# Other rows of the query weights in each partition, and a smaller step in the transposes of x

## The chip, the cores and the metric

The kernel runs on one core of a Trainium2 chip. The metric is the device time of one execution in microseconds; lower is better. The core has five engines with their own instruction streams: PE (matrix multiply, with its weight loads shown apart as PEld), DVE (vector), ACT (scalar), POOL (GpSimd) and SP, whose queue issues most of the transfers here.

## The reference

A block of new tokens attends to the last window of a key and value cache, with eight query heads for each head of keys and values. In sizes: x is 8 x 32 x 1024, the caches are 8 x 4 x 8192 x 128, of which the last W = 2048 positions are used, wq is 1024 x 4096 and wo is 4096 x 1024, all in bf16.

```python
q = (x @ wq).reshape(B, Sq, Hq, Dh).transpose(0, 2, 1, 3)
k = repeat(k_cache[:, :, Sk - W:, :], 8, axis=1)
v = repeat(v_cache[:, :, Sk - W:, :], 8, axis=1)
p = softmax(einsum("bhqd,bhkd->bhqk", q, k) * Dh ** -0.5)
o = einsum("bhqk,bhkd->bhqd", p, v)
out = o.transpose(0, 2, 1, 3).reshape(B, Sq, Hq * Dh) @ wo
```

## The kernel before

The attention is worked off in 32 units, one for each of 4 groups (a head of keys and values with its 8 query heads) and 8 batches. In each unit PE multiplies the transposed keys by the queries (line 504, 4 matmuls of 256 columns a step), ACT takes the exponential (line 506), and PE multiplies the result by the values, which carry an extra column of ones for the sum of the exponentials (line 515). Between these steps a plan written out by hand, in slots of a quarter of a unit, places the other work of PE: the queries of the next group (line 285), the transposes of keys, and the output projection (line 322). The order of instructions on each engine is that of the source; no scheduler moves them.

The contraction of x @ wq runs over the 1,024 columns of x. It is cut into 8 chunks of 128, one row of wq to a partition in each chunk. Any assignment of rows to chunks and partitions gives the same sum, as long as x is cut in the same manner. Before the change, partition p holds rows 8p to 8p+7 of wq: chunk c is row 8p+c. The weights of a group are loaded in two halves, chunks 0 to 3 and 4 to 7, each into its own tile `wq_sb` (`load_wq`, line 168). Every half is cut further into pieces of one or two chunks, each one transfer on SP's queue.

At the start (`start`, from line 340 on) the transfers go out in this order: x in two parts (SP and ACT), the first four chunks of group 0 one by one, chunks 4 and 5 together, half of the first keys, chunks 6 and 7 one by one, the other half of the keys, then values and further keys.

PE begins with eight warm-up matmuls on constants (line 375), since nothing has landed yet. It then transposes x in 16 blocks of 128 x 128 (`x_turn`, line 383, in two halves of 8), and two copies for each half, on DVE and ACT (line 386), bring them to `xT`. For each chunk, 8 matmuls (line 405, one for each head) follow, with 16 transposes of the first keys (line 397) before and after the last two chunks. Only then does the first unit start. The queries of half the batches for heads 4 to 7 are made a little later (line 301).

The transposes read x with a step, to match the rows of the weights: chunk c takes every eighth column, beginning at c.

```python
nc.tensor.transpose(ps[:, c, t, :], x_sb[:, t, half * H + c:self.D:self.DC], self.ident[:, :])
```

Here H is 4 and DC is 8. A weight load of PE takes these 128 columns, so that neighbours lie 8 elements, 16 bytes, apart in a partition.

Of the kernel before, what the change touches and what calls it, by code (L numbers as in the profile page):

```python
# [108 lines left out]
class Fast:  # L109
# [50 lines left out]
    def load_wq(self, g, half, cuts=(2, 2)):  # L160

        P, GW = self.P, self.rep * self.Dh

        def piece(i, n):
            if i == 0:
                self.wq_t[g, half] = self.wp.tile([P, self.DC // 2, GW], BF16, name="wq_sb", tag="w")
            c0 = half * self.DC // 2 + i
            self.nc.sync.dma_start(out=self.wq_t[g, half][:, i:i + n, :],  # L168
                                   in_=self.wq[:, g * GW:(g + 1) * GW].rearrange("(p c) n -> p c n", p=P)[:, c0:c0 + n, :])
        return [lambda i=sum(cuts[:k]), n=n: piece(i, n) for k, n in enumerate(cuts)]  # L170

    def load_wo(self, gq):
# [166 lines left out]
    def start(self):  # L339
        nc, P = self.nc, self.P  # L340
        warm = self.ps_s.tile([P, 512], FP32, name="warm_ps", tag="s_ps")
        one = nc.const_aps.tensor
        x_sb = self.vp.tile([P, self.NT, self.D], BF16, name="x_sb", tag="v")
        xf = self.x.rearrange("b s d -> (b s) d")
        H = self.DC // 2
# [33 lines left out]
        def x_turn(half, pl, tag):  # L379
            ps = pl.tile([P, H, self.NT, P], BF16, name="xT_ps", tag=tag)  # L380
            for c in range(H):
                for t in range(self.NT):
                    nc.tensor.transpose(ps[:, c, t, :], x_sb[:, t, half * H + c:self.D:self.DC], self.ident[:, :])
            for i, copy in ((0, nc.vector.tensor_copy), (1, nc.scalar.copy)):
                c0 = half * H + i * H // 2
                copy(out=self.xT[:, c0:c0 + H // 2, :], in_=ps[:, i * H // 2:(i + 1) * H // 2, :, :].rearrange("p c t s -> p c (t s)"))

        x_turn(0, self.ps_m, "m")
        x_turn(1, self.ps_s, "s_ps")
        qs = [self.ps_o.tile([P, 2, self.NQ], FP32, name="q0_ps", tag="o_ps") for _ in range(2)]  # L390
        qs.append(self.ps_m.tile([P, 4, P], FP32, name="q0_ps", tag="m"))
# [302 lines left out]
```

## Time and profile before

| | |
|---|---|
| median of 4 runs | 184.8 us (184.49 to 185.19) |
| profiled execution, its own time | 184.5 us |
| its span, first to last instruction | 182.7 us |
| DRAM read over the span | 41.42 MB, 230 GB/s |
| weights of the queries, transfers | 13 of 512 KB, 6 of 256 KB |
| transposes of x (line 383) | 16, first and last start at 4.4 and 5.8 us |
| first matmul of the queries (line 405) | 6.01 us |

The page gives, for each engine, its busy time, the share of the span and the number of instructions. PE and PEld overlap. The chain of waits follows the last instruction back to what released each step; in its pieces the first number is the start in us, the second the length. A row of windows shows the stretch, its length, the busy time of PE, PEld, DVE, ACT and POOL with the number of instructions, then the granted clock of PE, the DMA engines' share and GB/s. An issue row gives the size and the time from issue to landing.

### The profile page before, as it was taken

Reading aid. Unit: us, or ns where it says so; the run is one execution under the profiler, and the core shown is the slowest. Engines: PE = TensorE matmul, PEld = TensorE weight load, DVE = VectorE, ACT = ScalarE, POOL = GpSimd, SP = SyncE. Lnnn points to the kernel's source line nnn. Section 1 sums busy time; section 2 is a strip of 40 time slices with the busy share of each in tenths; the row PEclk is TensorE's granted clock in tenths of the full one; section 3 lists DMA queues with packets and bytes.
Section 4 is the critical chain, followed back from the end, with each engine's and each line's share of the span. In section 5 each row is a group of like instructions: output and inputs, shape, how many; then the busy total and the mean of one; then the engine's idle time right before and its main releaser. Section 6 shows DMA issues by size and latency. Waiting matters only on the chain.

```text
span 182.7 us, 5015 instructions
## 1 busy us (share of the span) xinstructions
PE 177.4 (97%) x2026; PEld 152.5 (83%) x2041; DVE 126.0 (69%) x257; ACT 136.0 (74%) x146; POOL 89.1 (49%) x138
## 2 busy tenths in 40 slices
PE   8989999999999999999999999999999999999993
PEld 2889999999999999998777899988787788888853
DVE  0228899679887698487799566777587987554253
ACT  2218898898897888997777787888877788888800
POOL 2004465069870795945939807929705949600000
PEclk9999999999999999999999999999999999999999
DMA  5999999999999999999999999999989999970013
GB/s 188 341 413 406 240 385 355 221 305 262 373 390 246 343 207 369 351 320 318 286 388 357 401 253 262 372 229 367 315 248 286 358 250 374 212 210 0 0 40 85
DMA packets 52954, 51.73 MB, mean 283 GB/s; under 512 B 39744, under 2 KB 40256, under 8 KB 52928
## 3 DMA queue, kind: packets, MB, share of 16 engines
q1 hardware_dynamic: 52352, 50.90, 97.9%
q10 hardware_dynamic: 576, 0.49, 0.9%
q8 instruction: 16, 0.26, 0.6%
q14 instruction: 10, 0.08, 0.1%
HBM read 41.42 MB, written 0.52 MB: 230 GB/s over the span
## 4 chain that ended last, share of the span: by engine, by line
PE 93%; DMA 4%; SPq 1%; issue 1%; DVE 0%
PE o_ps L515 32%; PE s_ps L504 31%; PE op_ps L322 14%; PE q_ps L285 11%; DMA wq_sb<-in_wq_dram 4%; PE q_ps L405 2%; PE ql_ps L301 1%; PE tp L244 1%; SPq L168 1%; PE kf_ps L397 0%; SPq L347 0%; DVE o_t L332 0%; PE cnt_ps L570 0%
## 5 line engine op out<-in xcount | busy, mean ns | idle before, releaser
L506 ACT ACTIVATE pT<-s_ps 128x1024 bf16<-128x1024 f32 x128 | 128.4, 1027 | 26.9 <-PE s_ps L504 26.7
L270 POOL TENSOR_SCALAR kTv<-kb 32x512 bf16<-32x512 bf16 x126 | 84.3, 669 | 51.6 <-DVE kb L259 33.4
L515 PE MATMUL o_ps<-va,pT 128*128 128x129 bf16 x1024 | 78.8, 220 | 0.1
L515 PEld LDWEIGHTS <-pT 128*128 128x128 bf16 x1024 | 68.5, 98 | 3.1
L504 PE MATMUL s_ps<-QT,kT 128*128 128x256 bf16 x336 | 50.4, 272 | 0.1
L504 PEld LDWEIGHTS <-kT 128*128 128x128 bf16 x336 | 31.9, 98 | 9.4
L322 PE MATMUL op_ps<-wo_sb,OT 128*128 128x512 bf16 (+2 forms) x129 | 32.8, 353 | 0.6
L259 DVE STREAM_TRANSPOSE kb<-k_raw 128x512 bf16<-128x512 bf16 x44 | 29.7, 692 | 1.1 <-DMA k_raw<-in_k_cache_dram 0.8
L285 PE MATMUL q_ps<-xT,wq_sb 128*128 128x256 bf16 x192 | 28.3, 273 | 0.0
L439 DVE COPY va<-v_sb 128x2048 bf16<-128x2048 bf16 x30 | 25.3, 844 | 2.0 <-DMA v_sb<-in_v_cache_dram 1.6
L504 PE MATMUL s_ps<-QT,kTv 128*128 128x256 bf16 x176 | 26.4, 273 | 0.1
L445 DVE RECIPROCAL RL_all<-o_ps 128x2 f32<-128x2 f32 x32 | 5.3, 166 | 26.8 <-PE o_ps L515 26.5
L268 DVE COPY kTv<-kb 32x512 bf16<-32x512 bf16 x50 | 22.7, 455 | 1.2
L504 PEld LDWEIGHTS <-kTv 128*128 128x128 bf16 x176 | 17.0, 98 | 6.1
L285 PEld LDWEIGHTS <-wq_sb 128*128 128x128 bf16 x192 | 16.9, 98 | 1.2
L451 DVE STREAM_TRANSPOSE OT<-o_sb 128x256 bf16<-128x256 bf16 x32 | 14.3, 446 | 1.1
L449 DVE TENSOR_TENSOR o_sb<-o_ps,RL_all 128x256 bf16<-128x256 f32 x32 | 13.6, 424 | 1.1
L322 PEld LDWEIGHTS <-OT 128*128 128x128 bf16 x144 | 11.4, 98 | 2.3 <-DVE OT L451 0.2
L437 POOL TENSOR_SCALAR va<-v_sb 128x2048 bf16<-128x2048 bf16 x2 | 3.8, 1897 | 17.2 <-DMA v_sb<-in_v_cache_dram 17.2
L288 ACT CAST QT<-q_ps 128x512 bf16<-128x512 f32 x12 | 7.0, 583 | 0.2 <-PE q_ps L285 0.2
L329 DVE TENSOR_TENSOR oacc<-op_ps,oacc 128x512 f32<-128x512 f32 x8 | 5.3, 662 | 2.0 <-PE op_ps L322 2.0
L405 PE MATMUL q_ps<-xT,wq_sb 128*128 128x256 bf16 (+1 forms) x64 | 5.8, 246 | 0.9 <-DMA wq_sb<-in_wq_dram 0.9
(35 smaller groups left out, 43.1 us busy)
## 6 DMA issues: line engine op xcount, KB each, us to landing
v_sb<-in_v_cache_dram SPq DMA_DIRECT2D x30, 512.0 KB, 6.8
wo_sb<-in_wo_dram SPq DMA_DIRECT2D x16, 512.0 KB, 6.7
wq_sb<-in_wq_dram SPq DMA_DIRECT2D x13, 512.0 KB, 6.6
k_raw<-in_k_cache_dram SPq DMA_DIRECT2D x13, 512.0 KB, 5.8
wq_sb<-in_wq_dram SPq DMA_DIRECT2D x6, 256.0 KB, 5.0
v_sb<-in_v_cache_dram SPq DMA_DIRECT2D x4, 256.0 KB, 5.0
kT<-in_k_cache_dram SPq DMA_TRANSPOSE x36, 7.3
k_raw<-in_k_cache_dram SPq DMA_DIRECT2D x2, 256.0 KB, 6.7
```

The costliest lines, as they stand in the source:

```text
L259: nc.vector.transpose(out=st["kb"][:, sl, :], in_=self.k_raw[ui][:, sl, :])
L268: nc.vector.tensor_copy(out=out, in_=in_)
L270: nc.gpsimd.tensor_scalar(out=out, in0=in_, scalar1=1.0, scalar2=1.0, op0=ALU.mult, op1=ALU.mult)
L285: nc.tensor.matmul(st[k][:, hl % 2, :], lhsT=self.wq_t[g, i][:, c % (DC // 2), hl * P:(hl + 1) * P], rhs=self.xT[:, c, :], start=(c == 0 a ...
L322: nc.tensor.matmul(ps[:, 0:w], lhsT=self.OT[:, gq, c, t * P:(t + 1) * P], rhs=self.wo_t[gq][:, c, n0:n0 + w], start=(k == 0), stop=(k == 7))
L405: nc.tensor.matmul(ps, lhsT=self.wq_t[0, c // H][:, c % H, h * P:(h + 1) * P], rhs=self.xT[:, c, 0:n], start=(c == 0 and h in (0, 2, 4)), ...
L439: self.nc.vector.tensor_copy(out=out, in_=in_)
L449: nc.vector.tensor_tensor(out=o_sb[:, :, :, :], in0=o_ps[:, :, 0:Dh].rearrange("p q (i c) -> p q c i", c=4), in1=rl[:, ui * QT_N:(ui + 1) ...
L451: nc.vector.transpose(out=self.OT[:, g * QT_N:(g + 1) * QT_N, :, b * self.Sq:(b + 1) * self.Sq], in_=o_sb[:, :, :, :])
L504: nc.tensor.matmul(s_ps[:, jj, :], lhsT=self.kT[ui][:, c * CJ + jj, :], rhs=q_u, start=True, stop=True)
L506: nc.scalar.activation(out=pT[:, :, :], in_=s_ps[:, :, :], func=ACT.Exp, bias=0.0, scale=self.scale)
L515: nc.tensor.matmul(o_ps[:, qt, 0:self.VW], lhsT=pT[:, jj, qt * P:(qt + 1) * P], rhs=va[:, j, 0:self.VW], start=(j == 0 and qt == 0), stop= ...
```

## The change

In each half of the weights (512 rows of wq), partition p takes rows 4p to 4p+3 of that half. Chunk c of half h is then row 512h + 4p + c, where it was row 8p + 4h + c. The columns of x follow: the transposes of half h read every fourth column of the 512 columns of that half, so neighbours in a weight load lie 8 bytes apart. A transfer still moves the same number of rows of 2 KB; the rows of two neighbouring partitions lie 32 KB apart in DRAM, where they were 64 KB apart. No instruction is added, removed or moved.

```diff
@@ load_wq, piece
-            c0 = half * self.DC // 2 + i
+            R = self.D // 2
             self.nc.sync.dma_start(out=self.wq_t[g, half][:, i:i + n, :],
-                                   in_=self.wq[:, g * GW:(g + 1) * GW].rearrange("(p c) n -> p c n", p=P)[:, c0:c0 + n, :])
+                                   in_=self.wq[half * R:(half + 1) * R, g * GW:(g + 1) * GW].rearrange("(p c) n -> p c n", p=P)[:, i:i + n, :])
@@ start, x_turn
-                    nc.tensor.transpose(ps[:, c, t, :], x_sb[:, t, half * H + c:self.D:self.DC], self.ident[:, :])
+                    nc.tensor.transpose(ps[:, c, t, :], x_sb[:, t, half * H * P + c:(half + 1) * H * P:H], self.ident[:, :])
```

## The prediction

> **What bounds the kernel now.** I read the page's busy shares first, then the chain of waits over the first 16 us, then PE's own waits, and last the transfers of the first 12 us one by one.
>
> ```profile
> PE 177.4 (97%) x2026; PEld 152.5 (83%) x2041; DVE 126.0 (69%) x257; ACT 136.0 (74%) x146; POOL 89.1 (49%) x138
> PE q_ps L405 <- DMA wq_sb<-in_wq_dram: 0.9, 1, 0.9
> 3.07 6.55 DMA wq_sb<-in_wq_dram
> 9.67 1.49 PE q_ps L405 x16
> 11.16 0.45 PE kf_ps L397 x8
> 11.61 1.32 PE q_ps L405 x16
> ```
>
> PE is busy 97% of the span. The second line is from the list of PE's waits, which has only one other entry, the 0.8 us before the warm-ups: one wait of 0.9 us for the query weights of group 0. From the third line on (chain of waits: start, length, what) the chain is a transfer until 9.62 us and PE work after that, to the end. So the time is the landing of one transfer (x chunks 4 and 5 of the first query weights, issued at 3.07) plus 173 us of PE work that the change does not touch. The change touches two things: how PE reads x in the 16 transposes, and which rows of DRAM the weight transfers read.
>
> **The transposes (line 383).** Rows of the timeline, PE's weight loads: start, length, what.
>
> ```profile
> 1.59 0.15 PEld L375 LDWEIGHTS <-const-bfloat16-1.0 128*128 128x128 bf16 x1 [0.28 <-issue]
> 2.02 0.15 PEld L375 LDWEIGHTS <-const-bfloat16-1.0 128*128 128x128 bf16 x1 [0.28 <-issue]
> ...
> 4.65 0.38 PEld L383 LDWEIGHTS <-x_sb 128*128 128x128 bf16 x3
> ...
> 5.50 0.34 PEld L383 LDWEIGHTS <-x_sb 128*128 128x128 bf16 x4
> ...
> 10.95 0.49 PEld L397 LDWEIGHTS <-k_raw 128*128 128x128 bf16 x8
> ...
> 6.01 2.80 PE L405 MATMUL q_ps<-xT,wq_sb 128*128 128x256 bf16 x32
> 9.67 1.05 PE L405 MATMUL q_ps<-xT,wq_sb 128*128 128x256 bf16 x10 [0.86 <-DMA wq_sb<-in_wq_dram]
> ...
> 141.46 0.86 PE op_ps L322 x4
> ```
>
> In the source's rows one load of x takes 164 ns (median), one of k_raw 98. Three loads of x in 0.38 us start (0.38 - 0.164)/2 = 0.108 us apart; the later four, overlapping, (0.34 - 0.15)/3 = 0.063; the eight of k_raw, contiguous, (0.49 - 0.098)/7 = 0.056. The change halves the step of x from 16 to 8 bytes. What is that worth? [...] The warm-up matmuls of 512 columns start 0.43 us apart (1.59, 2.02), while four of 512 columns late in the chain of waits (last line above) take 0.86 us, 0.215 each: PE ran at half pace until at least 4.3 us, although the profile's clock row shows 1.00 there. Half of 0.43 by a quarter of the columns is 0.108 for 128 columns, exactly what the early transposes show, and the same 16-byte step then runs at 0.063. The clock sets the early pace, not the step. [...]
>
> [...] The 32 matmuls of chunks 0 to 3 run from 6.01 to 8.81, and then PE waits 0.86 us. [...] Also the copies of xT move forward with the transposes and end in the same wait. Cost of this part: 0.
>
> **The weight transfers (line 168).** The number of transfers, their sizes, their order on SP's queue, the bytes per packet (2 KB, since a group is 1,024 of 4,096 columns) and the order of instructions on every engine stay the same. A one-row piece reads 128 packets; before they lie 64 KB apart over the whole 8 MB matrix, after 32 KB apart over one half of it. Whether DRAM minds is what no row shows directly, so I bound it. Each issue, with KB and us from issue to landing (issues start at 1.19, 1.66, 2.12, 2.60, 3.07, 3.55 for the first half of k_raw, 4.50, 4.87):
>
> ```profile
> wq_sb<-in_wq_dram SPq DMA_DIRECT2D x1, 256.0 KB, 3.8
> wq_sb<-in_wq_dram SPq DMA_DIRECT2D x1, 256.0 KB, 4.6
> wq_sb<-in_wq_dram SPq DMA_DIRECT2D x1, 256.0 KB, 4.8
> wq_sb<-in_wq_dram SPq DMA_DIRECT2D x1, 256.0 KB, 5.3
> wq_sb<-in_wq_dram SPq DMA_DIRECT2D x1, 512.0 KB, 6.5
> k_raw<-in_k_cache_dram SPq DMA_DIRECT2D x1, 256.0 KB, 6.7
> wq_sb<-in_wq_dram SPq DMA_DIRECT2D x1, 256.0 KB, 6.5
> wq_sb<-in_wq_dram SPq DMA_DIRECT2D x1, 256.0 KB, 6.8
> ...
> 5.00:6.00 1.00, 1.00 (x13) 0.92 (x12) 0.42 (x1) 0.01 (x1) 0.00 (x0) 1.00 0.91 285
> 10.00:11.00 1.00, 1.00 (x15) 0.94 (x13) 0.00 (x0) 0.00 (x0) 0.00 (x0) 1.00 1.06 412
> ```
>
> Landings: 5.0, 6.3, 6.9, 7.9, 9.6 (chunks 4 and 5), 10.3 (k_raw), 11.0, 11.6. The last steps, for k_raw, chunk 6 and chunk 7, are all near 0.67 us for 256 KB: the 64 KB pitch then costs nothing against k_raw's contiguous rows. But from 5.0 to 9.6, five such amounts landed in 4.6 us instead of 5 x 0.67 = 3.35: 1.25 us were lost at the start, and the two window rows (last columns: DMA share and GB/s) show it as 285 GB/s between 5 and 6 us against 412 at 10 to 11. The trace does not say whether the pitch, or simply the start, caused that. Ends: if the pitch caused all of it and 32 KB cures it, chunks 4 and 5 land 1.25 sooner, of which PE can use its 0.86 wait and about 0.1 of earlier start, so -0.95; if the new pattern makes the second half pay it again, +0.7 (below). I take 0, because chunks 6 and 7 have the pitch and pay nothing, so time since the start looks like the cause, not the address.
>
> The other 12 transfers of weights, 512 KB each, land well ahead: those of group 1 issued at 20.66 and 21.29 take 5.9 and 6.5 us, so they are there at 26.6 and 27.8, and the first matmul on them starts at 29.3. That is cover of 1.5 us; each would need to take a good half longer than it does before PE sees it.
>
> **The sum.** The profiled execution took 184.5 us, 182.7 of them span. Transposes 0, transfers 0, no instruction moved: 184.5 again, which stands 0.3 below the median of 184.8. My forecast on the median's scale is 184.8.
>
> **The rivals.**
>
> *The transfers get faster.* The weights' 1.25 us at the start are partly due to the 64 KB pitch. For: the loss falls on weights, and between 3 and 4 us, while x (contiguous) was still coming in, the windows show 383 GB/s. Against: chunks 6 and 7. Anything from 0.55 to 0.95 us comes off: 183.85 to 184.25, say 184.1. It cannot be more: at 8.8 PE is the bound.
>
> *The second half becomes a first read (slower).* Before, chunk c of any partition lies in the same 64 KB that chunk 0 touched, so half 1 reads neighbours of what was just read. After, half 1 is another 4 MB that nothing has touched. If being touched for the first time is what chunks 1 to 3 paid (6.9 and 7.9 against steps of 0.67: 2.9 us for three, 0.3 extra each), chunks 4 and 5 land about 0.6 later, and since PE has no cover there, every bit of it reaches the end; chunks 6 and 7 add 0.6 more against cover of 0.4 (chunk 6 lands at 11.0, and PE takes it after the keys' transposes, at 11.4), so 0.1 to 0.2 on top: +0.7 to +0.8, 185.5. It decides as soon as chunks 4 and 5 land later than 9.6, with no threshold; beyond 0.55 us it is measurable. Against: chunk 0 itself, the first touch of all, lands at 5.0, only 0.6 after x (0.74 + 3.7 = 4.4), so it shows no stretch.
>
> *The pitch hurts all weights (slower).* If 32 KB makes engines collide and each 512 KB takes twice its 1.3 us step, group 1 arrives 2.6 later against cover of 1.5: +1.1 there, with another +1 at the start: 187. Against: smaller pitch, nearer to the contiguous case.
>
> That the change does not do what it says I exclude: step and rows are plain in the source.
>
> **How the numbers follow.** What a measurement of this kernel can tell from no change is about 0.3%, 0.55 us (the four runs alone lie 0.7 apart). Forecast, nothing visible: 0.40, all within. Faster transfers: 0.30, faster. Second half paying again: 0.25; pitch hurting everywhere: 0.05; both slower. The range 183.9 to 185.7 takes in the whole of the gain, the forecast with its spread, and most of the first slower case; it leaves out the last and the far end of the one before. The likeliest case alone is 184.3 to 185.3.
>
> **What would show it.** Right: line 383's early loads still 0.107 apart and the late ones nearer 0.056, xT copied a little earlier, PE's wait for the weights before L405 grown by that much, and chunks 4 and 5 landing at 9.6 within 0.3. The faster rival: that wait gone and the transfer's piece in the chain ending near 8.8. The first slower one: the wait at 1.4 us or more, with the later landings spaced over 0.67. The last: waits of PE for wq_sb at line 285. My forecast is wrong if chunks 4 and 5 land over half a microsecond away from 9.6, or if early transposes drop to 0.06 and the time moves with them.

## The result and the profile after

The changed kernel takes 184.3 us in the median of 34 runs (183.64 to 186.31), the kernel before 184.88 in 55 runs of the same comparison. The ratio is 0.997, with a 95% interval of 0.9956 to 0.9983: 0.3% faster, at the edge of what I had called measurable, and I had forecast no visible difference. Three repeats of the same comparison gave less (1.0004, 0.9984, 0.9981). What follows is therefore about two questions: is it faster, and which of the two edits does it.

The page of the changed kernel, its busy line:

```profile
PE 177.4 (97%) x2026; PEld 152.4 (84%) x2041; DVE 125.9 (69%) x257; ACT 136.0 (75%) x146; POOL 89.3 (49%) x138
```

The same 177.4 us of PE: no work has become shorter. PE's list of waits, the entry for the weights:

```profile
PE q_ps L405 <- DMA wq_sb<-in_wq_dram: 0.3, 1, 0.3
```

The wait that was 0.9 is 0.3. The chain of waits of the changed kernel, at its start and its end (start, length, what):

```profile
3.08 5.98 DMA wq_sb<-in_wq_dram
9.11 1.49 PE q_ps L405 x16
...
175.36 3.94 PE op_ps L322 x34
```

and the last line's counterpart in the kernel before:

```profile
175.92 3.94 PE op_ps L322 x34
```

Chunks 4 and 5 land at 9.06 where they landed at 9.62. PE goes on at 9.11 instead of 9.67, 0.56 earlier, and the last block of the output projection also starts 0.56 earlier. In between nothing is lost and nothing is gained in these two executions (in two others of those below, part of such a gain is lost again). The span fell by 0.4 only (182.7 to 182.3), because the last stores took a little longer in this execution.

The issues of the changed kernel, in the order shown for before (size, us from issue to landing):

```profile
wq_sb<-in_wq_dram SPq DMA_DIRECT2D x1, 256.0 KB, 3.9
wq_sb<-in_wq_dram SPq DMA_DIRECT2D x1, 256.0 KB, 4.4
wq_sb<-in_wq_dram SPq DMA_DIRECT2D x1, 256.0 KB, 4.6
wq_sb<-in_wq_dram SPq DMA_DIRECT2D x1, 256.0 KB, 5.1
wq_sb<-in_wq_dram SPq DMA_DIRECT2D x1, 512.0 KB, 6.0
```

Chunks 1 to 5 each come 0.2 to 0.6 us sooner; the first does not. One window of the changed kernel (last columns: DMA share, GB/s):

```profile
5.00:6.00 1.00, 1.00 (x14) 0.90 (x12) 0.42 (x1) 0.02 (x1) 0.00 (x0) 1.00 1.05 397
```

Between 5 and 6 us, where before moved 285 GB/s, there are now 397. One such row proves little: the kernel with the old rows and the new step, shown below, moved 367 in the same microsecond. The transposes, on the other hand, give nothing to the end. From the source's rows of line 383 and the timeline:

```profile
L383 PEld LDWEIGHTS <-x_sb x16: 112/138/147, 4.4 to 5.7; 128*128 128x128 bf16 x16
```
```profile
4.37 1.64 PE L383 MATMUL xT_ps<-ident,x_sb 128*128 128x128 bf16 x16
6.00 2.80 PE L405 MATMUL q_ps<-xT,wq_sb 128*128 128x256 bf16 x32
```

A load is 26 ns shorter (138 against 164), the 16 transposes take 1.64 us instead of 1.69, and the first matmul of the queries starts at 6.00 instead of 6.01.

### The profile page after: what moved, and what is told of

Same layout as the page of the kernel before. It is cut to its first block, busy times and chain, and to the rows that moved or that the text cites. A ratio compares the mean times of both kernels' runs of the same rounds, so it can differ in the third digit from the quotient of the medians.

```text
span 182.3 us, 5015 instructions
## 1 busy us (share of the span) xinstructions
PE 177.4 (97%) x2026; PEld 152.4 (84%) x2041; DVE 125.9 (69%) x257; ACT 136.0 (75%) x146; POOL 89.3 (49%) x138
## 4 chain that ended last, share of the span: by engine, by line
PE 93%; DMA 3%; SPq 1%; issue 1%; DVE 0%
PE o_ps L515 32%; PE s_ps L504 31%; PE op_ps L322 14%; PE q_ps L285 12%; DMA wq_sb<-in_wq_dram 3%; PE q_ps L405 2%; PE tp L244 1%; PE ql_ps L301 1%; SPq L168 1%; PE kf_ps L397 0%; SPq L347 0%; DVE o_t L332 0%; PE cnt_ps L570 0%
```

## The experiments

**Each edit by itself.** One theory: the rows of DRAM carry the gain (R). A rival: PE reads x in 16-byte steps while the weights arrive, which holds the arriving data up, so the smaller step carries it (S). A third: there is no difference, only a start that jitters (N). Two kernels take one edit each, two more carry the idea of R further.

The rows alone:

```diff
-                   in_=self.wq[:, g * GW:(g + 1) * GW].rearrange("(p c) n -> p c n", p=P)[:, c0:c0 + n, :])
+                   in_=self.wq[half * R:(half + 1) * R, g * GW:(g + 1) * GW].rearrange("(p c) n -> p c n", p=P)[:, i:i + n, :])
```

> Only the DRAM rows of the weights change (partition p takes rows 4p to 4p+3 of each half); x is still transposed with step 8, so the queries are not those of the reference. If the rows carry the gain (theory R): ratio near 0.997, chunks 4 and 5 of group 0 land near 9.1 us, PE's wait before line 405 near 0.3 us. If the smaller step carries it (theory S: PE's reads of x with 16-byte steps hold up the arriving weights): ratio 1.000, chunks 4 and 5 land near 9.6.

The step alone:

```diff
-                    nc.tensor.transpose(ps[:, c, t, :], x_sb[:, t, half * H + c:self.D:self.DC], self.ident[:, :])
+                    nc.tensor.transpose(ps[:, c, t, :], x_sb[:, t, half * H * P + c:(half + 1) * H * P:H], self.ident[:, :])
```

> Only the step of x in the transposes changes from 8 to 4; the rows of the weights stay 8p to 8p+7, so the queries are not those of the reference. Theory R: ratio 1.000, chunks 4 and 5 land near 9.6, loads of x a little shorter with nothing gained. Theory S: ratio near 0.997 and chunks 4 and 5 near 9.1.

Partitions 8 KB apart:

```diff
-                   in_=self.wq[:, g * GW:(g + 1) * GW].rearrange("(p c) n -> p c n", p=P)[:, c0:c0 + n, :])
+                   in_=self.wq[:, g * GW:(g + 1) * GW].rearrange("(c p) n -> p c n", p=P)[:, c0:c0 + n, :])
-                    ... x_sb[:, t, half * H + c:self.D:self.DC] ...
+                    ... x_sb[:, t, (half * H + c) * P:(half * H + c + 1) * P] ...
```

> Chunk c takes rows 128c to 128c+127, so neighbouring partitions lie 8 KB apart in DRAM and x is transposed from contiguous columns. Theory R in the form that a smaller distance between partitions is better: chunks 4 and 5 land between 8.6 and 9.1, PE's wait gone or nearly so, ratio 0.995 to 0.997. Theory R in the form that only a distance of 64 KB or the span of 8 MB is bad: as the change, 0.997. Theory S: loads of x near 98 ns, ratio 0.997 or a little less. If each first touch of a new region costs: every chunk touches a new 1 MB, and landings of chunks 1 to 5 stay spread, ratio 0.998 to 1.001.

Partitions 16 KB apart (two rows of each quarter of 256 rows; x with step 2):

```diff
+            r0 = (half * self.DC // 2 + i) // 2 * 2 * P
-                   in_=self.wq[:, g * GW:(g + 1) * GW].rearrange("(p c) n -> p c n", p=P)[:, c0:c0 + n, :])
+                   in_=self.wq[r0:r0 + 2 * P, g * GW:(g + 1) * GW].rearrange("(p c) n -> p c n", p=P)[:, i % 2:i % 2 + n, :])
```

> In each quarter of 256 rows partition p takes rows 2p and 2p+1: neighbours 16 KB apart, x step 2. Smaller distance is better: between the change and the 8 KB kernel, ratio 0.995 to 0.997. First touch costs: near 0.998. Theory S: 0.997.

Measured: rows alone 1.000 (0.9983 to 1.0018), step alone 1.0003 (0.9991 to 1.0015), 16 KB 1.0027 (1.0007 to 1.0047), 8 KB 1.0085 (1.0055 to 1.0114). Neither edit showed the 0.3% by itself. In their traces chunks 4 and 5 landed at 9.09 with the rows alone, as R had it, but at 9.29 with the step alone, where R had 9.6 and S 9.1. And "closer is better" fell: both narrower patterns are slower. In the kernel with 8 KB, the first weights come a microsecond later than before (3.8 there), and the first row of its issues says so:

```profile
wq_sb<-in_wq_dram SPq DMA_DIRECT2D x1, 256.0 KB, 4.8
```

Weights behind the pair and the later keys are late too (PE's weight loads wait for weights twice, 0.7 and 0.3 us, where before has one such wait, and these keys land at 17.23), and PE gets a second wait for a transfer that before does not have (its list of waits; tp are the transposes of later keys):

```profile
PE tp L244 <- DMA k_raw<-in_k_cache_dram: 0.8, 1, 0.8
PE q_ps L405 <- DMA wq_sb<-in_wq_dram: 0.5, 1, 0.5
```

The step alone, by its trace, also answers what sets the pace of the transposes. Its timeline:

```profile
4.15 1.89 PE L383 MATMUL xT_ps<-ident,x_sb 128*128 128x128 bf16 x16
```

Sixteen transposes with the small step take 1.89 us here, longer than with the large step in before (1.69), and as much as the contiguous ones of the 8 KB kernel (1.91).

**Repeats, and the wait taken away.** The kernels before and after once more as they are, and both with chunks 4 and 5 of group 0 as two transfers, so that PE need not wait for the pair:

```diff
-        wq0 = self.load_wq(0, 0, (1, 1, 1, 1)) + self.load_wq(0, 1, (2, 1, 1))
-        for p in wq0[:5]:
+        wq0 = self.load_wq(0, 0, (1, 1, 1, 1)) + self.load_wq(0, 1, (1, 1, 1, 1))
+        for p in wq0[:6]:
             p()
         self.load_k(0, 0)
-        wq0[5]()
         wq0[6]()
+        wq0[7]()
```

> The kernel before, unchanged, against itself: how far a ratio strays by itself (1.000 within 0.002 expected by every theory), and a second trace of the start: chunks 4 and 5 land near 9.6 if theory R (rows) holds, anywhere between 9.0 and 9.6 if the landing only jitters (theory N).

> The changed kernel, unchanged, beside the others on one chip. Theory R: median span 0.3 us below that of before (as rows alone), ratio 0.997 to 0.9985, chunks 4 and 5 near 9.1. Theory N (no difference, start jitter): ratio 1.000, landing anywhere from 9.0 to 9.6.

> The kernel before, with chunks 4 and 5 of group 0 as two transfers of 256 KB. If PE's wait for the pair sets the time: chunk 4 lands about 0.67 us ahead of the pair, PE goes on with it, wait 0.1 to 0.3, ratio 0.996 to 0.998. If something else sets it, 1.000.

> The changed kernel with the same split. If the rows gain by shortening the same wait, little is left: its wait was 0.3, so the split brings at most 0.3 more, ratio to before 0.995 to 0.998, and no more than 0.1 us away from the split of before. If rows gain elsewhere, both gains add: 0.993 to 0.995.

Measured: before against itself 0.9998 (0.9982 to 1.0014), the changed kernel 1.0004 (0.9988 to 1.0021), split before 0.9997 (0.9983 to 1.0011), split after 0.9994 (0.9974 to 1.0014). So the 0.3% did not come back, and the trace of the repeat shows why one trace must not be trusted here. Timeline rows of the changed kernel, second execution:

```profile
4.08 1.07 PE L383 MATMUL xT_ps<-ident,x_sb 128*128 128x128 bf16 x16
7.57 2.15 PE L405 MATMUL q_ps<-xT,wq_sb 128*128 128x256 bf16 x24 [1.53 <-DMA wq_sb<-in_wq_dram]
10.24 1.49 PE L405 MATMUL q_ps<-xT,wq_sb 128*128 128x256 bf16 x16 [0.53 <-DMA wq_sb<-in_wq_dram]
```

The same program, with transposes of only 1.07 us, and yet chunk 1 came at 7.5 and chunks 4 and 5 at 10.2: its span was 183.3. The landing of this pair was at 9.62, 9.48, 9.29 and 9.24 in four traces with the old rows, and at 9.06, 10.20, 9.62, 9.18, 9.09 and 9.22 in six with the new ones. The means are 9.41 and 9.40: the scatter between executions is as large as the effect sought, and these ten traces alone show no difference.

Does a shift of the landing always reach the end? In eight of these ten traces the last block of the output projection starts 166.25 to 166.34 us after PE's first matmul on the pair. In two with the new rows it does not. In the fourth timing of the changed kernel (one of the further timings below) that matmul starts at 9.23, 0.44 earlier than in before, but the last block at 175.80, only 0.12 earlier; the second timing of the rows alone shows the same (9.27 and 175.78). A piece of the chain of waits of the former:

```profile
9.87 9.81 DMA k_raw<-in_k_cache_dram
19.71 0.71 DVE kb L259
...
22.04 0.61 PE s_ps L504 x4
```

A later load of keys lands at 19.68. DVE, which keeps the order of the source, rearranges these keys first (kb), and only afterwards copies the transposed keys of another unit to kT (line 246, at 21.4), for which PE waits until 22.04. In before the same step of DVE began at 19.37, which would let PE go on at 21.71, and PE came there only at 22.17. So there is a second gate, less than half a microsecond behind the first: an earlier landing of the pair counts in full only as far as these keys do not hold PE up.

The split did take the wait away. PE's row in the timeline of the split kernel with the old rows:

```profile
5.56 4.20 PE L405 MATMUL q_ps<-xT,wq_sb 128*128 128x256 bf16 x48
```

48 matmuls now run without a pause. The first exponential started 1.16 us earlier than in before (12.76 against 13.92), but by that of the third unit only 0.69 was left (22.18 against 22.87): the gates behind it, transfers of chunk 6 (PE takes it at 10.26, as soon as it has landed) and of the later keys (DVE waits 1.6 us for them) among them, take over. The 0.7 that was left did reach PE's last block, which starts at 175.22 instead of 175.92. But the span of this execution is 182.8, no shorter than that of before. Part of the reason stands at the very end, in SP's waits and signals (before, then the split kernel):

```profile
L689 SPq EVENT_SEMAPHORE  x10: 17/28/28, 180.4 to 182.7; - x10
L689 SPq EVENT_SEMAPHORE  x10: 17/28/28, 181.4 to 182.7; - x10
```

In before SP has seven of these ten behind it when the last store lands at 181.83, and the program ends 0.89 us later. In the split kernel SP begins with them only when the last store has landed, at 181.42, and the end comes 1.33 us later. The twelve traces of kernels without the split, before's among them, all have 0.89 or 0.90 there, and the other split kernel has 1.34. So both split kernels pay 0.45 us at the end that the others do not; that the one transfer more shifts the order of these waits is a guess. In time, then, the split is worth nothing that can be measured, and by the words of its expectation ("If something else sets it, 1.000") that would speak against the pair as the gate; but the test has this second effect, and with mean spans of 182.63 and 182.60 against 182.70 the two split kernels would be some 0.5 us ahead without it, an estimate. That the two are alike (0.03 ± 0.12 apart) is what the expectation asked for if the rows gain through this same wait.

**The transfers by themselves.** To get more than one start out of an execution, a kernel without any attention issues the seven weight transfers of the start again and again, each time after the last has drained, on 16 matrices of 8 MB in the caches that stand in for the weights. A second one deals the patterns to other matrices.

```python
pitch = (64, 32, 16, 8)[i % 4]      # second kernel: (32, 8, 64, 16)[i % 4]
for n in (1, 1, 1, 1, 2, 1, 1):     # chunks in a transfer, all on SP's queue
    nc.sync.dma_start(out=w[:, c:c + n, :], in_=rows(mat, pitch, c, n, c0))
```

> Only transfers, no attention; its time is not comparable. The seven transfers of the start (four of 256 KB, one of 512, two of 256) run on 16 matrices of 8 MB in the caches that stand in for the weights, with partitions 64, 32, 16 and 8 KB apart in turn (tiles far, half, quarter, near), each after the one before has drained; then all again on the next 2 KB of the same rows (tiles again). If 64 KB is what costs (theory R): the 512 KB piece of far lands 0.3 to 1 us later than that of half, in first and in again. If only narrow regions cost: near and quarter later, far and half alike. If a first touch costs: every first later than its again by 0.5 us or more. Theory N: spread of the four trials of one pattern (0.5 us or more) exceeds the difference between far and half.

> The same transfers with the patterns dealt to other matrices (half, near, far, quarter). A difference that belongs to the pattern stays with its name; one that belongs to the place in memory or in time moves.

From the first issue to the landing of the 512 KB piece, means of 16 trials of each pattern over both kernels: 7.53 us at 64 KB, 7.56 at 32, 8.62 at 16, 8.09 at 8 (standard errors of about 0.1). A row of the first kernel's issues for each (in the order 64, 32, 16, 8 KB; size, median us from its own issue):

```profile
again_far<-in_v_cache_dram SPq DMA_DIRECT2D x2, 512.0 KB, 5.7
again_half<-in_v_cache_dram SPq DMA_DIRECT2D x2, 512.0 KB, 5.5
again_quarter<-in_v_cache_dram SPq DMA_DIRECT2D x2, 512.0 KB, 6.8
again_near<-in_v_cache_dram SPq DMA_DIRECT2D x2, 512.0 KB, 6.5
```

These rows are of the matrices in v_cache, two trials each; in k_cache the row for 32 KB reads 6.8 and that for 64 KB 5.7, so that a single row says little. By the means the two narrow patterns are late, as in the timed kernels; only one of the four groups of four trials with 8 KB is not (7.72, against 7.83 with 64 KB in the same kernel and pass). 64 and 32 KB are alike. Rows touched for the first time were no slower than on the second pass (7.40 against 7.65 at 64 KB, 7.49 against 7.64 at 32), so the rival that I had built on first touches has nothing under it.

**More timings, and the whole start.** The change and each edit were timed again on other chips, and the whole start (x, weights, the first keys) was repeated by itself, the two patterns in turn, first on stand-ins:

```python
nc.sync.dma_start(out=xs[:, 0, :], in_=xf[0:P, :])
nc.scalar.dma_start(out=xs[:, 1, :], in_=xf[P:2 * P, :])
for n in (1, 1, 1, 1, 2, 0, 1, 1, 0):   # 0: a half of the first keys
    ...
```

> The changed kernel once more, on another chip if one is given. Theory R: mean span 0.2 to 0.3 us below that of before. Theory N: within 0.15 us of it, ratio within 0.998 to 1.002.

> The rows alone once more (x still with step 8, so the queries are not those of the reference). Theory R: mean span 0.2 to 0.3 us below that of before. Theory N: within 0.15 us.

> The changed kernel once more. If its true gain is what the spans of the earlier runs give, mean span 0.15 to 0.2 us below that of before and ratio 0.998 to 1.000; if it is the 0.3% first seen, 0.997 and 0.5 us.

> The step of x alone once more (rows as before, so the queries are not those of the reference). Mean span as before within 0.1 us, ratio 1.000; 0.15 us or more below it if the step, not the rows, carries the small gain.

> Only transfers, no attention; its time is not comparable. Each of 48 trials issues the whole start of the kernel, x in two parts, the seven weight transfers and the two halves of the first keys between them, with partitions 64 KB (rows_far) or 32 KB apart (rows_half) in turn, 24 trials each, on stand-ins for the weights in the caches. Theory R (32 KB lets chunks 4 and 5 land earlier): mean landing of the 512 KB piece 0.2 to 0.6 us earlier in rows_half. Theory N: the means differ by less than 0.15, the trials of one pattern spread over 1 us.

> The same with the two patterns exchanged between the matrices. Theory R: the difference stays with rows_half. Theory N: difference under 0.15 again, or of the other sign.

The timings: the change 0.9984 (0.9966 to 1.0002) and 0.9981 (0.9966 to 0.9997), rows alone 1.000 (0.998 to 1.002), step alone 1.0002 (0.9991 to 1.0013). The spans of the single runs scatter less than their times (for before, standard deviations of 0.32 to 0.34 us against 0.36 to 0.53 in four comparisons), but leave out the 2 us around them. Pooled over the chips (mean and its standard error; the first comparison has 36 spans on record for its 34 times):

| kernel | runs | mean span, us |
|---|---|---|
| before | 187 | 182.72 ± 0.02 |
| step alone | 36 | 182.67 ± 0.05 |
| rows alone | 36 | 182.49 ± 0.06 |
| the change, the three repeats | 58 | 182.50 ± 0.05 |
| the change, first comparison | 36 | 182.51 ± 0.07 |

So pooled, the change takes 0.22 ± 0.05 us off the span, 0.12%, the rows alone take off as much, and the step 0.05 ± 0.05. This is less firm than it looks, for two reasons. Taken comparison by comparison, each against before on the same chip, the change gives +0.02 ± 0.11, -0.25 ± 0.10 and -0.41 ± 0.09, which differ by more than these errors; the rows alone give -0.19 ± 0.10 and -0.21 ± 0.12; the step alone 0.01 ± 0.08 and -0.19 ± 0.09, and the second of these is beyond the 0.15 that its expectation had named as a sign for the step. And in the metric itself, the device time, the means over the same runs are 184.69 ± 0.03 for before, 184.51 ± 0.07 for the change, 184.65 ± 0.09 for the rows alone and 184.57 ± 0.05 for the step alone: the change gains 0.2, but which edit brings it the times do not show. For the rows speak the spans and the transfers by themselves.

The start on stand-ins gave half an answer: with 48 trials a pattern, chunk 3 landed at 6.83 with 32 KB and at 7.08 with 64, but the pair 4 and 5 at 8.43 and 8.49 (standard errors 0.05; all counted from the issue of x). The pair is what PE waits for, so this did not explain 0.22. The same kernel was then pointed at the real weights of group 0 and the real first keys (28 trials of each pattern), on two chips:

```diff
-                w = trial(..., mat, mats[(i + 5) % len(mats)], pitch, turn * GW)
+                w = trial(..., wq, None, pitch, 0)
```

> Only transfers, no attention; its time is not comparable. The start again, 28 trials of each pattern in turn, now on the real query weights of group 0 and the real first keys, so at the kernel's own addresses. The timed kernels say the rows gain 0.2 us. If that is chunks 4 and 5 landing earlier: rows_half 0.1 to 0.4 us earlier for the 512 KB piece, and its step after chunk 3 near 1.4 us against 1.7 or more in rows_far, as in the traces of the kernels. If the stand-ins were representative: under 0.15 apart, chunk 3 earlier by 0.25 in rows_half.

> Exactly the run before it again, on another chip if one is given. If the difference between the patterns belongs to the rows, it has the same sign and about the same size; if it belongs to where the matrix lies in one chip's memory, it changes.

The issues of the 512 KB pair, first run:

```profile
rows_far<-in_wq_dram SPq DMA_DIRECT2D x28, 512.0 KB, 6.3
rows_half<-in_wq_dram SPq DMA_DIRECT2D x28, 512.0 KB, 5.9
```

second run:

```profile
rows_far<-in_wq_dram SPq DMA_DIRECT2D x28, 512.0 KB, 6.3
rows_half<-in_wq_dram SPq DMA_DIRECT2D x28, 512.0 KB, 6.0
```

Counted from the first issue, that of x, the pair lands at 8.66 and 8.68 with 64 KB, at 8.30 and 8.45 with 32: 0.36 and 0.23 earlier, over both 8.67 against 8.38, a difference of 0.29 ± 0.07. The gain builds up over chunks 2, 3 and the pair (steps of 0.99, 0.96 and 1.50 us with 64 KB, 0.87, 0.80 and 1.44 with 32). Chunks 0 and 1 land no earlier, and chunk 6 follows in 1.34 and 1.38. So it is mostly chunks 2 and 3 that gain, not the pair's own step, which I had expected to do it (1.4 against 1.7). One thing was not varied here: 64 KB always had the first turn and 32 KB the second; only on the stand-ins were the two exchanged.

## Why the prediction was wrong

The frame held in the main. The time is the landing of chunks 4 and 5 plus fixed PE work, and no wait of PE on later weights (line 285) has appeared. But the PE work is fixed only as long as the later keys leave PE alone: in eight of ten traces a shift of the landing comes to the end within a tenth, in two about 0.3 of it is lost at that second gate. The prediction did not have it, and its end of -0.95 was too wide: with the wait for the pair gone altogether, in the split kernel, PE's last block came 0.70 earlier. No run shows the "about 0.1 of earlier start" in that end: the first matmul of the queries starts at 6.01 and 5.69 in two traces of before and at 6.00 and 5.22 in two of the change, and what differs there is the pace of the transposes, described next. A smaller slip, without effect: a cover of 1.5 us on transfers of 5.9 and 6.5 us lets the tighter one grow by a quarter, not by "a good half".

The transposes held too, as nothing on the path. The step alone gives a span of 182.67 ± 0.05 against 182.72. That the pace of PE and not the step makes the early transposes slow was an argument from one trace; now sixteen transposes with a step of 8 bytes have taken 1.07 to 1.98 us in seven executions, and contiguous ones 1.91. They start 0.107 us apart before the full pace and 0.056 after; with 16 bytes it is 0.107 and 0.063, so that the larger step costs nothing at half pace and 0.007 us a block at full pace. What differs between the executions is when the full pace began: from about 4.1 us, before the first transpose, to after the last. That it is the clock, as I wrote, no run shows: the windows' column for it reads 1.00 in the slow stretch and in the fast one. That the 16 transposes of the two traces shown first came down from 1.69 to 1.64 is luck: it is that moment which differs.

The step that failed is "The weight transfers": "I take 0, because chunks 6 and 7 have the pitch and pay nothing, so time since the start looks like the cause, not the address." I put the term at 0; it is -0.29 ± 0.07 us in the landing, by the transfers on the real weights, and -0.22 in the pooled span. Chunks 6 and 7 were the wrong witnesses. They come last in a queue and land in even steps in both patterns; their step of 0.67 says that nothing more is lost there, not that the pitch loses nothing before. In the transfers by themselves chunks 6 and 7 follow the pair in steps of 0.62 to 0.66 with every pitch, the slow ones of 16 and 8 KB too: such a step cannot tell one pitch from another. Of the 1.25 us that I found lost between chunk 0 and the pair, about a quarter (0.29) belongs to the 64 KB rows, an estimate that sets the transfers by themselves against one trace. The rest does not go with the pitch: the changed kernel's own trace still loses 0.64 there (9.06 - 5.07 = 3.99 against 3.35), and its second execution 1.81.

Of the rivals, "the transfers get faster" was right in mechanism, as far as the real weights show it, and too large in size: I gave it 0.55 to 0.95 us, and it is 0.2 to 0.3. First touches and a pitch that hurts everywhere both fell.

As to the number: the first comparison says 0.58 us between the medians, the pooled spans 0.22, the mean times of the three repeats 0.19 ± 0.07. In the four later comparisons with timings the median of before was 184.5 to 184.7, where the first had 184.88. The part beyond that did not come back, and no run here names a cause for it.

What stays open: how the gain in device time divides between the two edits; why rows 32 KB apart do better than 64 on the weights but not, for the pair, on the stand-ins, and why 16 and 8 KB do worse than both. The runs show that the result goes with place and pitch, not the rule behind it.

## What to carry to other kernels

Where one early transfer gates an engine that hardly idles afterwards, its landing can go into the time nearly one to one (here within 0.1 us in eight of ten traces), until the next gate takes over; here that was less than half a microsecond behind. Look for the next gate before promising the gain. Judge the pattern of a load by the transfer that is waited for, not by others of the same shape further back in the queue. When the effect is smaller than the scatter of a start, repeat the start many times inside one kernel and at the real addresses; one trace of each kernel would have put the start of PE's last block anywhere from 0.6 us earlier to 0.7 later here. And when an experiment takes a wait away and the time does not move, follow the gain through the trace to where it is lost: here to another wait and to the end of the program.

## What the runs showed of the hardware that I had not expected

Rows that lie closer together in DRAM did not always load faster: in the transfers by themselves the 512 KB pair landed at 7.5 to 7.6 us with partitions 64 and 32 KB apart, at 8.1 with 8 KB and at 8.6 with 16 KB. The order is not even monotone.

PE runs the 16 transposes of x, with the same step of 8 bytes, in 1.07 to 1.98 us, depending on when its full pace begins (0.107 us from one to the next before, 0.056 after), while the windows' column for the granted clock says 1.00 throughout.

The same start of the same program lets one transfer of 256 KB land 1.0 us after the one before it in one execution (5.07 to 6.06) and 2.5 in another (5.04 to 7.52).
